# Decoding the first MLP's weight chunks in whole instead of in halves

## The chip, the cores and the metric

The kernel runs on one core of a Trainium2 chip. The metric is the device time of one execution in microseconds (us), given as the median of the runs.

## What is computed

Attention with a decay over 4 x 8 heads of 576 positions and 64 columns, whose output (2304 tokens x 512) goes through two MLPs. The inputs of the weights are float64.

```python
x = np.ascontiguousarray(attn_out.transpose(0, 2, 1, 3)).reshape(B * S, H * D)
# first MLP: w_in is 512 x 2048, w_out is 2048 x 512
h = x @ w_in
g = h - np.tanh(h)
x = g @ w_out
# second MLP: the same sizes
h = x @ w_in
r = np.maximum(h, 0.0)
out = (r * r) @ w_out
```

## The kernel before

Matrix products are made from a high and a low part of each operand (`PASSES`: high x high, high x low, low x high), so every operand is split: ScalarE rounds it to the high part, and a subtraction on VectorE or GpSimd gives the low part.

The first MLP's weights come in 16 chunks of 128 hidden columns. `load_w` brings a chunk with two DMAs on SyncE's queue: the w_in columns into the first half of the tile `wraw`, the w_out rows into the second half, as pairs of 32-bit words, two words for each float64. `decode_w` makes float32 numbers of them and then the two parts, in `w`. It works by halves of 512 numbers, first the w_in half (x = 0), then the w_out half (x = 1):

- `first(x)`: two ScalarE operations (L203, L204) take every second word each and shift it by a multiplication;
- `bits(x)`: two VectorE operations (L210, L212) put the fraction, the exponent and the sign together in the half of `wfull`;
- `parts(x)`: ScalarE makes the high part (L227), then the low part is made (L228) by GpSimd for the w_in half and by VectorE for the w_out half.

The tile `w` takes the place of `wraw`, so no part can be written before the last `bits` operation has read from there. `wfull` comes from a pair of buffers of 1024 columns (`wide`).

Order: the program is emitted by a clockwork. Each `cw.step` emits one piece of TensorE work (an atom) and counts one tick; `cw.later(k, fn)` emits `fn` k ticks later. `first(0)`, then 2 ticks (`LAG['wbits']`) to `bits(0)` and `first(1)`, 2 ticks to `bits(1)`, 3 ticks (`LAG['wparts']`) to `parts(0)`, 1 tick to `parts(1)`: 8 ticks for a chunk. A planner then orders the instructions of each engine, mainly by the order of emission, and places the semaphores; an engine runs its own list in order. A chunk's decode is begun by `feed.pace`, by how far TensorE's atoms of the first block of tokens are, or by `feed.upto` when a step of that block needs it. Before `h1_atoms` emits products with a chunk that is not in `ready_w`, it steps the clock until it is. The h products (L1017) read the w_in half (`win`), high part first; the y products (L1057) read the w_out half (`wout`).

In the same stage the first half of the attention's heads runs: GpSimd makes the decay rows Pb (L552, L556), VectorE takes the row maximum (L669), ScalarE the exponential (L678).

The second MLP's weights go through the same function with phase 1 and 2, later in the span.

Of the kernel before, what the change touches and what calls it, by code (L numbers as in the profile page):

```python
# [10 lines left out]
F32 = mybir.dt.float32  # L11
F32R = mybir.dt.float32r
U32 = mybir.dt.uint32
AF = mybir.ActivationFunctionType
ALU = mybir.AluOpType
# [4 lines left out]
NT, DM, DFF = B * S, H * D, 2048  # L20
P = 128
# [36 lines left out]
LAG = dict(max=2, exp=1, norm=3, tr=3, trlo=2, pv=1, pvadd=1, qk=1, qklo=1, th=1, sub=1, hi=1, lo=1, wbits=2, wparts=3,  # L58
           relu=1, sq=1, lo2=1, load=8)
# [51 lines left out]
def fused_kernel(ctx: ExitStack, tc: tile.TileContext, q, k, v, f, w1i, w1o, w2i, w2o, out):  # L111
    nc = tc.nc
    cw = Clockwork(tc)
# [3 lines left out]
    wp = ctx.enter_context(tc.tile_pool(name="wp", bufs=1))  # L117
# [15 lines left out]
    wraw, wt, ready_w = {}, {}, set()  # L133
# [12 lines left out]
    def pin(ins):  # L146
        if ordered:
            tc.keep_in_program_order(ins)
# [4 lines left out]
    def wide(name, dtype):  # L153
        return wp.tile([P, 1024], dtype, tag="wide", name=name, bufs=2)

    def load_w(phase, fc):
        if phase == 0:
            t = wp.tile([P, 2, 1024], U32, tag=f"w{fc}", name=f"wraw_{phase}_{fc}", bufs=1)
            src_in, src_out = wsrc[0]
            pieces = ((t[:, 0].rearrange("p (c f) -> p c f", c=ND),  # L160
                       src_in[:, 2 * fc * P : 2 * (fc + 1) * P].rearrange("(c p) f -> p c f", p=P)),
                      (t[:, 1], src_out[fc * P : (fc + 1) * P, :]))
        else:
            tag = SUMTAG[fc] if phase == 1 else 15
            t = wp.tile([P, 2, 1024], U32, tag=f"w{tag}", name=f"wraw_{phase}_{fc}", bufs=1)
            src_in, src_out = wsrc[1]
            if phase == 1:
                pieces = [(t[:, c].rearrange("p (c f) -> p c f", c=2),
                           src_in[2 * c * P : 2 * (c + 1) * P, 4 * fc * P : 4 * (fc + 1) * P]
                           .rearrange("(c p) f -> p c f", p=P)) for c in range(2)]  # L170
            else:
                pieces = [(t[:, c], src_out[(2 * fc + c) * P : (2 * fc + c + 1) * P, :]) for c in range(2)]
        wraw[phase, fc] = t
        for dst, src in pieces:
            (move if phase == 2 else load)(dst, src)
# [3 lines left out]
    def decoded():  # L179
        busy.pop()  # L180
        if pending:
            decode_w(*pending.pop(0))

    pending = []

    def decode_w(phase, fc):
        if phase:
            if busy:
                pending.append((phase, fc))
                return  # L190
            busy.append((phase, fc))
        raw = wraw.pop((phase, fc)).rearrange("p i d -> p (i d)")
        pair = raw.rearrange("p (d t) -> p d t", t=2)
        full = wide(f"wfull_{phase}_{fc}", U32)
        w = 512

        spots = ((full[:, :w], full[:, w:]), (raw[:, :w], raw[:, w : 2 * w]))

        def first(x):
            lo_, hi_ = spots[x]  # L200
            words = pair[:, x * w : (x + 1) * w]

            pin(nc.scalar.activation(lo_, words[:, :, 0], AF.Copy, scale=0.936 * 2.0 ** -29))  # L203
            pin(nc.scalar.activation(hi_.bitcast(F32), words[:, :, 1].bitcast(F32), AF.Copy, scale=2.0 ** -112))  # L204
            cw.later(LAG['wbits'], lambda: bits(x))

        def bits(x):
            lo_, hi_ = spots[x]
            dst = full[:, x * w : (x + 1) * w]
            nc.vector.scalar_tensor_tensor(lo_, in0=hi_, scalar=3, in1=lo_,  # L210
                                           op0=ALU.logical_shift_left, op1=ALU.bitwise_or)
            nc.vector.scalar_tensor_tensor(dst, in0=hi_, scalar=0x80000000, in1=lo_,  # L212
                                           op0=ALU.bitwise_and, op1=ALU.bitwise_or)
            if x == 0:
                first(1)
            else:
                if phase == 2 and fc + 1 < NP2:
                    cw.later(1, lambda: load_w(2, fc + 1))
                cw.later(LAG['wparts'], (lambda: parts(0)) if phase == 0 else (lambda: combine(phase, fc, full)))

        def parts(x):
            if x == 0:
                wt[phase, fc] = wp.tile([P, 2, 2, DM], F32R, tag=f"w{fc}", name=f"w_{phase}_{fc}", bufs=1)
            t = wt[phase, fc]
            hi, lo = (t[:, hl].rearrange("p i d -> p (i d)")[:, x * w : (x + 1) * w] for hl in range(2))
            src = full[:, x * w : (x + 1) * w].bitcast(F32)
            nc.scalar.activation(hi, src, AF.Copy)  # L227
            (nc.vector if x else nc.gpsimd).tensor_tensor(lo, in0=src, in1=hi.bitcast(F32), op=ALU.subtract)  # L228
            if x == 0:
                cw.later(1, lambda: parts(1))  # L230
            else:
                ready_w.add((phase, fc))

        first(0)
# [880 lines left out]
    class Feed:  # L1115
# [11 lines left out]
        def one(self):  # L1127
            assert self.decoded < self.loaded
            decode_w(*self.items[self.decoded])
            self.decoded += 1  # L1130
# [164 lines left out]
    for fn, what in (  # L1295
            (lambda p: decode_w(2, p), {0: 20, 1: 34, 2: 48, 3: 62, 4: 76, 5: 90, 6: 104, 7: 118}),
            (lambda i: stage_load(i), {1: 9, 2: 64}),
            (lambda i, x: y_sum(i, x), {(1, 0): 22, (1, 1): 25, (1, 2): 32, (1, 3): 36,
                                        (2, 0): 75, (2, 1): 79, (2, 2): 89, (2, 3): 93}),
            (lambda p: final_load(p), {0: 121, 1: 122, 2: 134, 3: 141, 4: 148, 5: 150, 6: 152, 7: 172}),  # L1300
            (lambda p: final_split(p), {0: 128, 1: 136, 2: 143, 3: 148, 4: 157, 5: 168}),
            (lambda n: g_load(n), {0: 138, 1: 145, 2: 165, 3: 170}),
            (lambda n: g_sums(n), {0: 146, 1: 154, 2: 171}),
            (lambda hl: g_split_first(hl), {0: 159, 1: 161}),
            (lambda e: g_split_second(e), {0: 165, 1: 167})):
        for arg, at in what.items():
            events.setdefault(at, []).append((fn, arg))
# [250 lines left out]
```

## Time and profile before

| | |
|---|---|
| median of 3 runs | 1008.18 us (1006.85 to 1009.23) |
| the profiled execution | 1005.81 us |
| its span in the trace | 1004.1 us |
| TensorE busy | 977.4 us |
| VectorE busy | 722.0 us |
| ScalarE busy | 627.1 us |
| GpSimd busy | 356.3 us |
| HBM traffic over the span | 140 GB/s |

PE is TensorE's matmul, PEld its weight load, DVE is VectorE, ACT ScalarE, POOL GpSimd, SP SyncE. Busy time is the time in which an engine had an instruction in work; instructions that follow one another directly overlap a little, so two durations add up to more than the time from the first start to the second end. An idle time stands with the instruction that ended it and with what released that instruction.

### The profile page before, as it was taken

To read this page: it belongs to the slowest core of one execution; us is meant where nothing else is said; L and a number is where in the kernel's file an instruction comes from. 1 tells how busy PE (TensorE), PEld (TensorE's weight loads), DVE (VectorE), ACT (ScalarE), POOL (GpSimd) and SP (SyncE) were. 2 spreads that over 40 slices of the span, in tenths; PEclk is the share of its full clock that TensorE was granted. 3 is DMA by queue.
4 is the path that set the end of the run, shared out by engine and by line. 5 is a ranking of instruction groups with operands and counts; after the bars stand their busy time and mean duration, and the time that the engine had idled before them with its cause. 6 is when DMAs were issued, how large, how long until landed. Compare 5 with 4: busy or idle time off the path is not lost.

```text
span 1004.1 us, 19916 instructions
## 1 busy us (share of the span) xinstructions
PE 977.4 (97%) x6990; PEld 929.5 (93%) x6990; DVE 722.0 (72%) x1513; ACT 627.1 (62%) x1249; POOL 356.3 (35%) x511
## 2 busy tenths in 40 slices
PE   7989999999999999999999999999999999999998
PEld 5778889999999999999999877999999999999998
DVE  4897884587878877878753589755447569987773
ACT  5896874566666666665643367767666767655551
POOL 4664453455566655565510343342323000000000
PEclk9999999999999999999999999999999999999999
DMA  8946744363353444443201432576877974544431
GB/s 235 272 137 228 217 112 100 107 140 82 101 142 91 115 120 102 113 120 93 75 20 36 153 127 84 162 258 222 282 272 247 331 229 118 168 141 134 127 106 42
DMA packets 220004, 149.58 MB, mean 149 GB/s; under 512 B 116384, under 2 KB 197600, under 8 KB 219904
## 3 DMA queue, kind: packets, MB, share of 16 engines
q1 hardware_dynamic: 219856, 148.28, 50.3%
q8 instruction: 55, 0.90, 0.4%
q14 instruction: 45, 0.37, 0.1%
q10 hardware_dynamic: 48, 0.03, 0.0%
HBM read 101.00 MB, written 39.92 MB: 140 GB/s over the span
## 4 chain that ended last, share of the span: by engine, by line
PE 68%; DVE 10%; ACT 3%; issue 2%; DMA 1%; SPq 1%; POOL 1%; DVEq 0%; ACTq 0%; POOLq 0%
PE o L1394 17%; PE r L1226 15%; PE h L1017 14%; PE y L1057 14%; PE pv L858 3%; PE pt L775 2%; DVE KL L630 2%; PE s L740 2%; DVE PT L785 2%; PE s L742 1%; DVE Pb L669 1%; DVE g L1030 1%; DVE ghl L1038 1%; DVE wq L321 1%; PE pv L820 1%
## 5 line engine op out<-in xcount | busy, mean ns | idle before, releaser
L1057 PE MATMUL y<-ghl,w 128*128 128x256 f32 (+1 forms) x1536 | 241.2, 301 | 1.5 <-DVE ghl L1038 1.5
L1057 PEld LDWEIGHTS y<-ghl,w 128*128 128x128 f32 x1536 | 209.5, 191 | 13.4 <-DVE ghl L1038 3.3
L1017 PE MATMUL h<-x,w 128*128 128x256 f32 x1344 | 199.2, 291 | 5.5 <-POOL w L228 4.7
L1017 PEld LDWEIGHTS h<-x,w 128*128 128x128 f32 x1344 | 175.9, 192 | 12.8 <-POOL w L228 6.3
L1394 PE MATMUL o<-ws,gc 128*128 128x256 f32 x864 | 116.0, 283 | 0.0
L1394 PEld LDWEIGHTS o<-ws,gc 128*128 128x128 f32 x864 | 109.2, 192 | 0.0
L1226 PE MATMUL r<-yt,ws 128*128 128x384 f32 x576 | 106.6, 336 | 0.5 <-ACT g L1244 0.5
L1226 PEld LDWEIGHTS r<-yt,ws 128*128 128x128 f32 x576 | 100.0, 188 | 2.9 <-ACT g L1244 2.5
L1394 PE MATMUL o<-wq,gc 128*128 128x256 f32 x648 | 90.9, 284 | 1.7 <-DVE gc L1360 1.5
L694 POOL TENSOR_SCALAR Pb<-Pb,st 128x384 f32<-128x384 f32 (+2 forms) x80 | 58.0, 726 | 81.1 <-DVE st L688 60.7
L1394 PEld LDWEIGHTS o<-wq,gc 128*128 128x128 f32 x648 | 83.5, 192 | 2.5 <-DVE gc L1360 1.9
L669 DVE CUSTOM_DVE_ANT_0 Pb<-s,Pb 128x128 f32<-128x128 f32 (+4 forms) x144 | 66.9, 482 | 22.1 <-PE s L742 13.8
L678 ACT ACTIVATE Pb<-Pb,st 128x384 f32<-128x384 f32 (+2 forms) x80 | 55.2, 689 | 42.8 <-DVE st L669 42.0
L1226 PE MATMUL r<-yt,wq 128*128 128x384 f32 x432 | 80.1, 335 | 0.3 <-ACT g L1244 0.2
L1030 DVE TENSOR_TENSOR g<-h,g 128x512 f32<-128x512 f32 x72 | 49.4, 686 | 42.5 <-ACT g L1027 41.8
L1360 DVE TENSOR_TENSOR gc<-graw,gc 128x1792 fp32r<-128x1792 f32 x34 | 68.7, 2022 | 13.5 <-ACT gc L1356 13.5
L1226 PEld LDWEIGHTS r<-yt,wq 128*128 128x128 f32 x432 | 75.1, 188 | 1.3 <-ACT g L1244 1.1
L1356 ACT ACTIVATE gc<-graw 128x1792 fp32r<-128x1792 f32 x34 | 57.7, 1697 | 28.0 <-PE o L1394 17.6
L256 POOL TENSOR_TENSOR wsum<-wfull 128x256 f32<-128x256 f32 x32 | 29.9, 935 | 118.5 <-DVE wfull L212 95.3
L1237 DVE TENSOR_TENSOR g<-r,g 128x384 f32<-128x384 f32 x71 | 39.0, 553 | 42.3 <-PE r L1226 23.3
L1027 ACT ACTIVATE g<-h 128x512 f32<-128x512 f32 x72 | 42.7, 592 | 40.2 <-PE h L1017 39.6
L1034 ACT ACTIVATE ghl<-g 128x512 fp32r<-128x512 f32 x72 | 45.4, 630 | 34.6 <-DVE g L1030 33.9
(155 smaller groups left out, 1879.1 us busy)
## 6 DMA issues: line engine op xcount, KB each, us to landing
graw<-gscr SPq DMA_DIRECT2D x144, 128.0 KB, 2.6
gscr<-g SPq DMA_DIRECT2D x95, 192.0 KB, 3.6
wraw<-in_moe_w_in_dram SPq DMA_DIRECT2D x32, 512.0 KB, 4.6
wraw<-in_moe_w_out_dram SPq DMA_DIRECT2D x32, 512.0 KB, 5.5
neg<-cscr SPq DMA_DIRECT2D x32, 288.0 KB, 3.4
v<-in_v_dram SPq DMA_DIRECT2D x48, 128.0 KB, 2.8
qk<-in_k_dram SPq DMA_DIRECT2D x64, 72.0 KB, 2.4
K<-K SPq DMA_DIRECT2D x32, 144.0 KB, 3.0
```

Source lines behind the costliest of these rows:

```text
L669: nc.vector.tensor_tensor_reduce(out=d, in0=t[:rows, src : src + m], in1=d, scale=-0.125, scalar=3.0e38 if j == 0 else stat(0, x)[:rows], ...
L678: nc.scalar.activation(d, d, AF.Exp, bias=stat(len(parts) - 1, x)[:rows], scale=-1.0, accum_out=stat(2, x)[:rows])
L694: nc.gpsimd.tensor_scalar(d, d, r, 1.0, op0=ALU.mult, op1=ALU.mult)
L1017: nc.tensor.matmul(o, lhsT=win(fc, wh, dc), rhs=xpart(j, dc, xh), start=dc == 0 and wh + xh == 0, stop=dc == ND - 1 and wh == 1)
L1027: pin(nc.scalar.activation(g, t, AF.Tanh))
L1030: pin(nc.vector.tensor_tensor(g, t, g, op=ALU.subtract))
L1034: pin(nc.scalar.activation(ghl[:, 0], g, AF.Copy))
L1057: nc.tensor.matmul(o, lhsT=wout(fc, wh, i * P, P), rhs=ghl[:, xh, fj * n : fj * n + n], start=s == 0 and fj == 0 and wh + xh == 0 and i % ...
L1226: nc.tensor.matmul(t, lhsT=wprod(1, p, k, wh)[:, dc * P : (dc + 1) * P], rhs=yt[i, k][:, xh, dc], start=k in FRESH and dc == 0 and wh + xh ...
L1356: pin(nc.scalar.activation(hi, t[:, 1:8], AF.Copy))
L1360: pin(nc.vector.tensor_tensor(lo, in0=t[:, 1:8], in1=hi.bitcast(F32), op=ALU.subtract))
L1394: nc.tensor.matmul(o, lhsT=gc[n][gh, e][:, GWHERE[k]] if n == 1 else gc[n][gh][:, GWHERE[k], e], rhs=wprod(2, 2 * q + e, k, wh), start=q = ...
```

## The change

The first MLP's chunks go through a new function, `decode_first`; `decode_w` keeps the second MLP's. A chunk is decoded in whole: two ScalarE operations of 1024 columns read every second word of the whole tile (the second one writes into the tile's own first half), two VectorE operations of 1024 put the bits together, one ScalarE operation of 1024 makes the high part, and one tick later both low parts are emitted, GpSimd's for the first 512 columns and VectorE's for the last 512. The ticks are 2, 3 and 1.

```diff
+    def decode_first(fc):
+        raw = wraw.pop((0, fc)).rearrange("p i d -> p (i d)")
+        words = raw.rearrange("p (d t) -> p d t", t=2)
+        full, hi_ = wide(f"wfull_0_{fc}", U32), raw[:, :1024]
+        nc.scalar.activation(full, words[:, :, 0], AF.Copy, scale=0.936 * 2.0 ** -29)
+        nc.scalar.activation(hi_.bitcast(F32), words[:, :, 1].bitcast(F32), AF.Copy, scale=2.0 ** -112)
+
+        def bits():
+            nc.vector.scalar_tensor_tensor(full, in0=hi_, scalar=3, in1=full,
+                                           op0=ALU.logical_shift_left, op1=ALU.bitwise_or)
+            nc.vector.scalar_tensor_tensor(full, in0=hi_, scalar=0x80000000, in1=full,
+                                           op0=ALU.bitwise_and, op1=ALU.bitwise_or)
+            cw.later(LAG['wparts'], parts)
+
+        def parts():
+            t = wt[0, fc] = wp.tile([P, 2, 2, DM], F32R, tag=f"w{fc}", name=f"w_0_{fc}", bufs=1)
+            hi, lo = (t[:, hl].rearrange("p i d -> p (i d)") for hl in range(2))
+            src = full.bitcast(F32)
+            nc.scalar.activation(hi, src, AF.Copy)
+
+            def low():
+                for eng, c in ((nc.gpsimd, slice(0, 512)), (nc.vector, slice(512, 1024))):
+                    eng.tensor_tensor(lo[:, c], in0=src[:, c], in1=hi[:, c].bitcast(F32), op=ALU.subtract)
+                ready_w.add((0, fc))
+            cw.later(1, low)
+        cw.later(LAG['wbits'], bits)
+
     def decode_w(phase, fc):
+        if phase == 0:
+            return decode_first(fc)
```

## Rows read from the trace of the kernel before

**Rows 1.** The page: busy time (share, instructions), and PEld in 40 slices, tenths.

```profile
PE 977.4 (97%) x6990; PEld 929.5 (93%) x6990; DVE 722.0 (72%) x1513; ACT 627.1 (62%) x1249; POOL 356.3 (35%) x511
...
PEld 5778889999999999999999877999999999999998
```

**Rows 2.** Stretches: length, busy us (instructions) of PE, PEld, DVE, ACT, POOL; clock, DMA, GB/s.

```profile
42.00:133.00 91.00, 84.84 (x606) 75.20 (x604) 79.14 (x177) 73.84 (x178) 47.89 (x58) 0.94 0.63 194
...
150.00:175.00 25.00, 25.00 (x215) 24.53 (x213) 12.08 (x31) 12.13 (x31) 7.02 (x15) 1.00 0.45 97
...
50.00:58.00 8.00, 4.85 (x34) 3.80 (x33) 7.86 (x15) 8.00 (x21) 7.40 (x9) 0.99 0.41 113
58.00:66.00 8.00, 7.91 (x50) 7.45 (x51) 8.00 (x17) 6.43 (x16) 2.53 (x3) 0.79 0.43 142
```

**Rows 3.** Waits of PEld, 42 to 134 us: us in total, times, longest.

```profile
PEld h L1017 <- POOL w L228: 6.3, 7, 1.6
...
PEld h L1017 <- ACT w L227: 1.5, 3, 0.8
```

**Rows 4.** Timeline, chunks 14 and 15: start, us, engine, line, operation [idle before].

```profile
124.74 0.70 ACT L203 ACTIVATE wfull<-wraw 128x512 uint32<-128x512 uint32 x1
...
126.92 0.69 DVE L212 SCALAR_TENSOR_TENSOR wfull<-wfull 128x512 uint32<-128x512 uint32 x1
126.98 1.78 POOL L228 TENSOR_TENSOR w<-wfull,w 128x512 fp32r<-128x512 f32 x1 [2.95 <-ACT w L227]
...
127.53 1.78 DVE L228 TENSOR_TENSOR w<-wfull,w 128x512 fp32r<-128x512 f32 x1
...
131.16 1.16 ACT L227 ACTIVATE w<-wfull 128x512 fp32r<-128x512 f32 x2 [0.17 <-DVE wfull L212]
...
131.87 1.28 POOL L228 TENSOR_TENSOR w<-wfull,w 128x512 fp32r<-128x512 f32 x1 [0.54 <-ACT w L227]
...
132.35 1.35 DVE L228 TENSOR_TENSOR w<-wfull,w 128x512 fp32r<-128x512 f32 x1 [0.60 <-ACT w L227]
...
133.20 0.89 PEld L1017 LDWEIGHTS h<-x,w 128*128 128x128 f32 x7 [0.77 <-POOL w L228]
```

**Rows 5.** The decode's operations up to 140 us: ns min/median/max, first and last start.

```profile
L227 ACT ACTIVATE w<-wfull x32: 612/622/641, 25.4 to 131.7; 128x512 fp32r<-128x512 f32 x32
L203 ACT ACTIVATE wfull<-wraw x16: 642/670/697, 12.5 to 124.7; 128x512 uint32<-128x512 uint32 x16
...
L210 DVE SCALAR_TENSOR_TENSOR wfull<-wfull x16: 670/686/878, 13.8 to 126.1; 128x512 uint32<-128x512 uint32 x16
...
L228 POOL TENSOR_TENSOR w<-wfull,w x14: 1276/1416/1780, 46.3 to 131.9; 128x512 fp32r<-128x512 f32 x14
...
L228 DVE TENSOR_TENSOR w<-wfull,w x16: 679/834/1781, 27.9 to 132.3; 128x512 fp32r<-128x512 f32 x16
...
  DMA wraw<-in_moe_w_in_dram: 4.2, 2
```

**Rows 6.** 1024-wide operations elsewhere in the span, by line and shape: busy us, mean ns.

```profile
L1336 ACT ACTIVATE graw<-graw 128x1024 f32<-128x1024 f32 x36 | 38.0, 1057 | 38.1 <-DMA graw<-gscr 38.1
...
L320 ACT ACTIVATE ws<-wst 128x1024 fp32r<-128x1024 f32 x5 | 5.3, 1055 | 0.0
L321 DVE TENSOR_TENSOR ws<-wst_s,ws 128x1024 fp32r<-128x1024 f32 x3 | 3.7, 1221 | 1.5 <-ACT ws L320 1.5
```

**Rows 7.** Chunk 8: the issues on the timeline, us to landing, ScalarE's first operation.

```profile
62.98 0.45 SPq L140 DMA_DIRECT2D wraw<-in_moe_w_in_dram  x1
...
63.48 0.82 SPq L140 DMA_DIRECT2D wraw<-in_moe_w_out_dram  x1
...
wraw<-in_moe_w_in_dram SPq DMA_DIRECT2D x1, 512.0 KB, 7.9
wraw<-in_moe_w_out_dram SPq DMA_DIRECT2D x1, 512.0 KB, 8.7
...
71.02 0.69 ACT L203 ACTIVATE wfull<-wraw 128x512 uint32<-128x512 uint32 x1 [0.36 <-DMA wraw<-in_moe_w_in_dram]
```

## The prediction

> **What bounds the kernel now.** I read the page first: TensorE is busy for 97% of the span and its weight loads for 93%, but the loads stand at five to eight tenths in the first six of forty slices and then at nine, but for three slices around 600 us [rows 1]. So most of what another engine can still give back lies in the first 150 us, and the changed function works only there, from 12.5 us to 133 us [rows 5]. Next come the stretches. From 42 us (about where the first MLP's products begin) to 133 us (the last chunk is ready) TensorE's loads are busy 75.2 of 91 us, against 24.53 of 25 just behind; VectorE is busy 79.1 and ScalarE 73.8 of the 91, the granted clock is 0.94 of its full level, and in 50 to 66 us VectorE has nothing free at all (7.86 and 8.00 of 8.00) [rows 2]. So this stage is bound by a mesh: ScalarE and VectorE nearly full, and TensorE waiting for what they hand over.
>
> How much of that waiting is the decode's? In the same stretch the weight loads of the h products stand idle 6.3 us for GpSimd's low parts (seven times) and 1.5 us for ScalarE's high parts (three times) [rows 3]. These 7.8 us are what the change can reach directly.
>
> **One chunk, as it runs now.** Chunk 15: ScalarE starts it at 124.74, GpSimd's low part starts at 131.87 and takes 1.28, the product starts at 133.20 [rows 4]. That is 8.4 us to the end of the low part. With each operation at its own duration and nothing in the way: two ScalarE halves 1.21 (1.16 for two high parts back to back, and 0.05 more, since a half that reads every second word takes 0.67 against 0.62), two VectorE halves 1.29 (126.92 to 127.53 is 0.61 from start to start, plus 0.68), both again for the second half, a high part 0.62, the low part 1.28 [rows 4, 5]: 6.9 us. The other 1.5 us are queues at five hand-overs.
>
> **Part 1, wider operations.** The change makes three ScalarE operations of 1024 out of six of 512, two VectorE bit operations out of four, and leaves the low parts at 512. A 1024-wide copy on ScalarE takes 1.06 in two groups, two halves back to back 1.16 [rows 4, 6]: 0.10 us saved per pair, 0.3 a chunk, 4.8 over 16. For the pairs that read every second word I keep the 0.05 more for the whole too. On VectorE a 1024-wide operation with two inputs takes 1.22 undisturbed [rows 6], two halves 1.29: 0.07 saved per pair, 0.14 a chunk, 2.2 over 16. No row has a 1024-wide bit operation; the halves cost the same as a 512-wide subtraction (0.68), so the range is 0 to 0.14 per pair. Taken on an engine that is full, this is worth its sum at most: 14 chunks fall between 46 and 133 us, so 4.2 us of ScalarE and 2.0 us of VectorE [rows 5].
>
> **Part 2, a shorter chain.** The new chain, with nothing in the way: two whole ScalarE operations 2.1, two whole VectorE operations 2.4, high part 1.06, low part 1.28: 6.8 us, as good as the 6.9 now. What goes is two of five hand-overs, each worth 0.3 us by chunk 15: 0.9 left instead of 1.5, so a chunk is ready 0.7 us sooner. The emission says the same in its own unit: 2+2+3+1 = 8 ticks now, 2+3+1 = 6 then, so in the program a chunk's end stands two steps ahead of where it stood. But a product's first matmuls need only the high part, and that now comes as one operation of 1.06, not of 0.62: for the three waits on ScalarE 0.26 of the 0.7 is left. Taking 0.7 from each of the seven waits on GpSimd gives 4.9; not each is that long (0.9 on average, 1.6 the longest [rows 3]), so 4.5. With 0.26 from each of the three on ScalarE, 0.8, it is 5.3 us of 7.8.
>
> This sum isn't all kept. TensorE that is early by one wait meets the next chunk early too, and a chunk is started by ScalarE and VectorE, so what accumulates is limited by what these engines get ahead: 2.0 us on VectorE, 4.2 on ScalarE. Between 2.0 and 5.3 I take the middle, 3.6.
>
> **Part 3, both low parts at once.** The rows say they don't run at once. At 127.53 VectorE's low part was issued while GpSimd's ran until 128.76: it took 1.78 instead of 0.68 and ended 0.55 after GpSimd. At 132.35 the same: 1.35, and 0.55 after GpSimd's 133.15. The other way round, GpSimd's at 126.98 took 1.78 instead of 1.28, because VectorE's bit operation had begun at 126.92 [rows 4]. So whoever comes second stands still, and the pair takes 1.28 + 0.55 = 1.83 us from its release in either order. The Trainium skill states the mechanism (SBUF — State Buffer, Who interferes with whom): VectorE with two SBUF inputs and a GpSimd operation that reads SBUF share one port pair, under an exclusive lock that the first one keeps for its whole instruction. The trace agrees with it (1.78 against 0.68). If they could run side by side, a chunk's low parts would be ready 0.55 us sooner than in the sum made here.
>
> The cost: VectorE's low part has a minimum of 0.68, a median of 0.83 and a maximum of 1.78 [rows 5]. Issued beside GpSimd's every time, it lies between -0.15 (VectorE always first) and +0.95 us per chunk (always second) from the median: -2 to +13 us of VectorE over 14 chunks. I take +0.3, nearer the median, because when VectorE is behind with its queue some other operation of two inputs is the one that stands still, as now. That is 4 us of VectorE time against 2.0 saved; it counts where VectorE has nothing free, which the rows show for 16 of the 91 us: 16/91 of 4, 0.7 us. Where VectorE comes first, GpSimd's low part and the product behind it are late by 0.5; that is in the range.
>
> **Part 4, the first operation waits for both loads.** Now the first half reads only the w_in rows, the second only the w_out rows. A whole needs both. Chunk 8: w_in is issued at 62.98 and lands 7.9 later, at 70.9, and ScalarE, which waited for it, starts at 71.02; w_out is issued at 63.48 and lands after 8.7, at 72.2 [rows 7]. ScalarE would stand still 1.2 us more there, with the softmax's exponentials and the tanh behind it. Two waits on such loads show in all [rows 5]. I take 0 for these, since ScalarE has 17 us free in the stretch [rows 2], and keep 1.2 each, 2.4 us, for the range.
>
> What is moved besides: the wide buffer and the raw tile are freed two ticks sooner, and no DMA, semaphore queue or order of loads changes. The order within each engine follows from the order of emission and a planner, so the rest of the span shifts a little as well; no row bounds this, I allow 2 us either way.
>
> **Sum.** 3.6 - 0.7 = 2.9, about 3 us off the span: 1004.1 to 1001.1. The profiled execution took 1005.81 (1.7 beyond its span) and would take 1002.8; the median of the runs, 1008.18, lies 2.4 above it, so the median becomes 1005.2.
>
> **The rivals.**
> *More than that.* All 7.8 us of waits vanish, and with them part of what the lowered clock costs: 0.94 over 91 us is 5.5 us at the full level, and the deepest drop, 0.79 of 8 us, follows directly on the longest standstill, 50 to 58 us, where TensorE was busy only 4.85 of 8 [rows 2]. With 2 of the 5.5 us: 10 us, 998. Against it: ScalarE and VectorE can't get 10 us ahead.
> *Nothing.* The waits change their name. VectorE is full in 50 to 66, its own load hardly falls (2 saved, up to 4 added), and TensorE waits for the ghl or x parts instead of w. 1008, within 2. For it: VectorE is the fuller of the two engines; against it: 7.8 us of idle time have w as their releaser.
> *Slower.* The port pair. If VectorE's low part is second nearly always, it costs 0.95 a chunk, 13 us over the 14, less 2.0: 11 us, against 11.9 us that VectorE has free in the stretch [rows 2], and these are not free where needed. Half of it reaching TensorE gives 5.5 us, 1013.5. It decides from about 0.5 us a chunk on (7 us less 2.0 on VectorE, half of it 2.5, as much as the forecast gains), that is a mean low part of 1.3 us.
> That the change doesn't do what it says (no overlap) is part 3, and in all four cases.
>
> **How the numbers follow.** Forecast (about 1005.2, from 1001 to 1006) 0.40; more 0.10; nothing 0.26; slower 0.24. The range from 999.5 to 1012 leaves out the far ends of the first and the last rival. A measurement of this kernel tells 0.2% (2 us) from no change; with that bound the cases give faster 0.50, same 0.26, slower 0.24.
>
> **What would show it.** Right: the last low part ends before 132.5 instead of 133.15; the h products' idle time for w falls from 7.8 to about 3; ScalarE's busy time in the stage falls by 4 us or more; 1024-wide operations at 1.06 to 1.11 and 1.22. Part 3: VectorE's w low parts at a mean of about 1.1 to 1.3; at 1.6 the slower rival holds. Part 4: waits of ScalarE for the w_out load, where none is now. Wrong: the idle time for w falls and the last chunk is no sooner, or the difference arises behind 133 us, where the planner's order and not the decode made it.

## The result: slower by 0.8%

The changed kernel takes 1016.49 us (median of 7 runs, 1013.19 to 1018.38) against 1009.23 us for the kernel before on the same chip (7 runs, 1006.85 to 1013.92). The ratio is 1.0076, with a 95% interval from 1.0057 to 1.0095. The forecast was 1005.2 us, the range ended at 1012: the sign was wrong. The profiled execution took 1017.04 us with a span of 1014.9, 10.8 us more than the span of before; that is more than the ratio's 7.7, since the profiled execution of before (1005.81) was faster than its seven. An execution more than 1.5% above the fastest of its kernel is in no ratio below (two of ten in e6, four of ten in e8, one of twelve each in e14 and e15); with them the means put e6 and e14 at 0.995 and e8 at 1.010.

Each execution also has a mean granted clock of TensorE, and the time goes with it. Beside the experiments the kernel before took 1010.1 us on average at 0.990 (12 executions) and 1009.7 at 0.991 (20). The kernel after took 1015.17 at 0.990 and 1013.37 at 0.991. So 4 to 5 us of the loss are there at the same clock, and the rest comes with a lower one.

The page of the kernel after, its busy times and two of its rows of 40 slices (the answer to [rows 1]):

```profile
PE 986.4 (97%) x6990; PEld 937.2 (92%) x6990; DVE 718.4 (71%) x1481; ACT 622.5 (61%) x1201; POOL 357.3 (35%) x511
...
PEld 5778879999899999999999877899999999999998
...
PEclk9779999999999999999999999999999999999999
```

VectorE and ScalarE have less to do by 3.6 and 4.6 us, as the change intends, and the span is longer all the same. The stretches of [rows 2], and one more (same columns):

```profile
42.00:133.00 91.00, 83.59 (x562) 74.04 (x563) 68.72 (x141) 62.99 (x125) 44.02 (x55) 0.89 0.60 184
150.00:175.00 25.00, 25.00 (x212) 24.07 (x212) 14.76 (x45) 13.54 (x40) 6.20 (x15) 1.00 0.46 108
50.00:58.00 8.00, 6.59 (x52) 5.78 (x53) 7.69 (x17) 5.59 (x9) 4.05 (x4) 1.00 0.64 189
58.00:66.00 8.00, 5.84 (x29) 4.66 (x28) 7.56 (x10) 6.82 (x14) 4.24 (x5) 0.75 0.11 29
...
34.70:48.40 13.70, 13.70 (x57) 10.90 (x56) 8.89 (x30) 8.21 (x23) 7.25 (x16) 0.50 0.95 268
```

From 42 to 133 us TensorE gets through 562 matmuls instead of 606, with the clock at 0.89 instead of 0.94, and every helper engine is emptier. Nobody is full; they wait for one another.

Where the 10.8 us arise can be read off the h products on the timeline. The first one starts at 46.2 us (before: 42.0). From there to the 192nd, the last of the first block of tokens, it takes 99.0 us (before: 92.3). From there to the last h product of the first MLP it takes 498.1 (before: 497.0). So 4.2 us are lost before the first product, 6.7 in the stage in which the chunks are decoded, and almost nothing behind it. In that stage the weight loads stand idle 18.4 us instead of 14.2; the rest is slower work, with the clock at its lower level for 17.1 us of the stage instead of 10.2. In this execution the start has the clock at 0.50, its 1.2 GHz level, from 34.7 to 48.4 us (last row above).

What the weight loads of h wait for, in the kernel after from 42 to 145 us (the answer to [rows 3]; engine and line, releaser: us in total, times, longest):

```profile
PEld h L1046 <- POOL w L208: 7.8, 8, 2.9
...
PEld h L1046 <- ACT w L204: 2.2, 2, 1.7
```

That is 10.0 us instead of 7.8, and the longest wait for GpSimd is 2.9 instead of 1.6. So 2.2 of the 4.2 us of added idle time have w as their releaser. The decode's operations in the kernel after, up to 150 us (ns min/median/max, as in [rows 5]):

```profile
L190 ACT ACTIVATE wfull<-wraw x16: 1108/1143/1187, 14.6 to 133.9; 128x1024 uint32<-128x1024 uint32 x16
...
  DMA wraw<-in_moe_w_out_dram: 1.0, 1
...
L204 ACT ACTIVATE w<-wfull x16: 1041/1056/1060, 27.3 to 140.5; 128x1024 fp32r<-128x1024 f32 x16
...
L194 DVE SCALAR_TENSOR_TENSOR wfull<-wraw,wfull x16: 1197/1226/1843, 18.2 to 136.3; 128x1024 uint32<-128x1024 uint32 x16
...
L208 POOL TENSOR_TENSOR w<-wfull,w x16: 1264/1494/1944, 28.4 to 141.7; 128x512 fp32r<-128x512 f32 x16
L208 DVE TENSOR_TENSOR w<-wfull,w x16: 671/692/1776, 34.6 to 141.6; 128x512 fp32r<-128x512 f32 x16
```

The widths cost what was forecast. VectorE's low part got no longer: over 42 to 145 us its mean is 1.04 us, against 1.05 before. GpSimd's own duration is little longer (1.54 us in the mean, 1.46 before). What is late, in some chunks, is its start. One chunk of the kernel after, number 11 (the first is 0), rows of its timeline (the chunk's first operation is at 104.00; the operations at 110.00 and 111.74 are the next chunk's, and the row at 114.01 holds the low parts of both chunks, 1.26 us the first):

```profile
104.00 1.15 ACT L190 ACTIVATE wfull<-wraw 128x1024 uint32<-128x1024 uint32 x1
105.54 1.13 ACT L191 ACTIVATE wraw<-wraw 128x1024 f32<-128x1024 f32 x1
105.58 0.82 POOL L581 TENSOR_SCALAR Pb<-neg,ccol 128x128 f32<-128x128 f32 x2
...
106.76 1.23 DVE L194 SCALAR_TENSOR_TENSOR wfull<-wraw,wfull 128x1024 uint32<-128x1024 uint32 x1 [0.57 <-ACT wraw L191]
...
108.50 1.22 DVE L196 SCALAR_TENSOR_TENSOR wfull<-wraw,wfull 128x1024 uint32<-128x1024 uint32 x1
...
109.80 1.05 ACT L204 ACTIVATE w<-wfull 128x1024 fp32r<-128x1024 f32 x1
...
110.00 1.23 DVE L194 SCALAR_TENSOR_TENSOR wfull<-wraw,wfull 128x1024 uint32<-128x1024 uint32 x1
...
111.14 0.69 DVE L208 TENSOR_TENSOR w<-wfull,w 128x512 fp32r<-128x512 f32 x1
...
111.56 2.00 POOL L581 TENSOR_SCALAR Pb<-neg,ccol 128x128 f32<-128x128 f32 x2 [4.68 <-DMA neg<-cscr]
...
111.74 1.22 DVE L196 SCALAR_TENSOR_TENSOR wfull<-wraw,wfull 128x1024 uint32<-128x1024 uint32 x1
...
113.64 0.41 POOL L585 TENSOR_SCALAR_AFFINE_SELECT Pb<-Pb 128x256 f32<-128x256 f32 x1
...
114.01 2.97 POOL L208 TENSOR_TENSOR w<-wfull,w 128x512 fp32r<-128x512 f32 x2
...
115.33 1.24 PEld L1046 LDWEIGHTS h<-x,w 128*128 128x128 f32 x10 [2.92 <-POOL w L208]
```

The high part is done at 110.85. GpSimd's low part starts 3.2 us later, because two decay rows and a select stand ahead of it on its queue. Three things add up: the decay rows wait for their own load (`neg`) until 111.56, 0.7 us; they take 2.00 us (0.82 where nothing holds them, at 105.58), while VectorE's three operations with two inputs from 110.00 to 112.96 follow one another without a gap; and the select takes the rest. So 1.2 of the 3.2 us are time in which GpSimd is held, and 2.0 are its queue. TensorE stands 2.92 us for it. The chunk takes 11.3 us from its first operation to the end of its low part.

This does not happen to every chunk. Of chunks 2 to 15, ten have GpSimd's low part done 1.35 to 2.03 us behind the high part, as before (1.36 to 1.98). Four are late: 5.5 and 2.5 us (chunks 7 and 8), 4.4 and 2.9 (11 and 12). In chunk 7, too, decay rows that had waited for their load stand ahead; the first of them takes 2.83 us. The low parts of 8 and 12 stand behind those of 7 and 11:

```profile
81.36 3.28 POOL L581 TENSOR_SCALAR Pb<-neg,ccol 128x128 f32<-128x128 f32 x2 [2.09 <-DMA neg<-cscr]
...
85.09 2.52 POOL L208 TENSOR_TENSOR w<-wfull,w 128x512 fp32r<-128x512 f32 x2
```

Chunk 7's lateness cost TensorE 0.17 us, since its products were not due yet; the 2.92 us for chunk 11 are the one wait for GpSimd in this trace that is longer than the longest of before (1.6).

The kernel before, the chunk at the same place, the ScalarE and VectorE rows of its timeline:

```profile
113.03 0.67 ACT L203 ACTIVATE wfull<-wraw 128x512 uint32<-128x512 uint32 x1
113.60 0.65 ACT L204 ACTIVATE wfull<-wraw 128x512 f32<-128x512 f32 x1
...
114.67 0.68 ACT L203 ACTIVATE wraw<-wraw 128x512 uint32<-128x512 uint32 x1
...
114.91 0.69 DVE L210 SCALAR_TENSOR_TENSOR wfull<-wfull 128x512 uint32<-128x512 uint32 x1
...
115.23 0.68 ACT L204 ACTIVATE wraw<-wraw 128x512 f32<-128x512 f32 x1
```

Here VectorE joins the bits of the first half (114.91) while ScalarE reads the second (114.67 to 115.91). That overlap inside a chunk is gone in the kernel after. Taken over chunks 2 to 15, a chunk's mean time from its first ScalarE operation to the end of its w_in low part is 9.36 us before and 11.37 after: 7.72 and 9.08 to the end of the w_in high part, 1.64 and 2.29 from there.

### The profile page after: what moved, and what is told of

It is laid out like the page before. It is cut to its first block, busy times and chain, and to the rows that moved or that the text cites. A ratio compares the mean times of both kernels' runs of the same rounds, so it can differ in the third digit from the quotient of the medians.

```text
span 1014.9 us, 19817 instructions
## 1 busy us (share of the span) xinstructions
PE 986.4 (97%) x6990; PEld 937.2 (92%) x6990; DVE 718.4 (71%) x1481; ACT 622.5 (61%) x1201; POOL 357.3 (35%) x511
## 4 chain that ended last, share of the span: by engine, by line
PE 67%; DVE 13%; issue 6%; ACT 5%; POOL 3%; DMA 3%; SPq 1%; POOLq 0%; DVEq 0%; ACTq 0%
PE o L1423 16%; PE h L1046 14%; PE y L1086 13%; PE r L1255 12%; PE pv L887 3%; PE pt L804 2%; PE s L769 2%; DVE PT L814 2%; DVE KL L659 2%; PE s L771 1%; DVE g L1059 1%; DVE ghl L1067 1%; DVE Pb L698 1%; POOL w L208 1%; POOL Pb L581 1%
## 5 line engine op out<-in xcount | busy, mean ns | idle before, releaser
L1086 PE MATMUL y<-ghl,w 128*128 128x256 f32 (+1 forms) x1536 | 244.3, 303 | 1.5 <-DVE ghl L1067 1.5
L1086 PEld LDWEIGHTS y<-ghl,w 128*128 128x128 f32 x1536 | 211.9, 193 | 13.6 <-DVE ghl L1067 3.3
L707 ACT ACTIVATE Pb<-Pb,st 128x384 f32<-128x384 f32 (+2 forms) x80 | 55.2, 690 | 42.9 <-DVE st L698 42.2
```

The costliest lines, as they stand in the source:

```text
L707: nc.scalar.activation(d, d, AF.Exp, bias=stat(len(parts) - 1, x)[:rows], scale=-1.0, accum_out=stat(2, x)[:rows])
L1086: nc.tensor.matmul(o, lhsT=wout(fc, wh, i * P, P), rhs=ghl[:, xh, fj * n : fj * n + n], start=s == 0 and fj == 0 and wh + xh == 0 and i % ...
```

## The experiments

Two theories stood at the beginning. S: the loss is made at the start, by chunks 0 and 1, and by the lowered clock there. P: every whole chunk costs, by the port pair (in the forecast's slower rival, by VectorE's low part being held) and by longer operations ahead of others. The traces of e1 and e3 brought a third. Q: the other side of the same lock, GpSimd held by VectorE's operations, its low part late and h waiting. Its rival O, named with e5: the order that the planner makes for whole chunks is worse in itself, and GpSimd only shows it. All ratios are to the kernel before on the same chip (e1 to e4 and e13 to e16 ran on one chip, e5 to e12 on another), with 95% intervals.

| label | kernel | ratio | interval |
|---|---|---|---|
| e1 | after, chunks 0 and 1 in halves | 1.0081 | 1.0048 to 1.0114 |
| e2 | before, chunks 0 and 1 in whole | 1.0029 | 1.0010 to 1.0048 |
| e3 | after, more filling matmuls | 1.0103 | 1.0062 to 1.0143 |
| e4 | before, more filling matmuls | 0.9966 | 0.9943 to 0.9988 |
| e5 | after, the two low parts swapped | 1.0029 | 1.0010 to 1.0049 |
| e6 | after, both low parts on VectorE | 0.9962 | 0.9925 to 0.9999 |
| e7 | after, each 1024 as two 512 | 1.0058 | 1.0022 to 1.0094 |
| e8 | after, bit operations a tick apart | 1.0034 | 1.0013 to 1.0054 |
| e9 | before, both low parts on VectorE | 1.0002 | 0.9983 to 1.0022 |
| e10 | before, both low parts in one tick | 0.9976 | 0.9954 to 0.9998 |
| e11 | after, low parts a tick apart | 1.0099 | 1.0065 to 1.0133 |
| e12 | e6, more filling matmuls | 0.9985 | 0.9966 to 1.0005 |
| e13 | e6, GpSimd's subtraction back, unread | 1.0090 | 1.0058 to 1.0122 |
| e14 | e6 again | 0.9943 | 0.9926 to 0.9961 |
| e15 | e6, an unread GpSimd subtraction, 12 chunks | 1.0035 | 1.0015 to 1.0054 |
| e16 | as e15, on the chunk before | 1.0014 | 0.9992 to 1.0037 |

### Is it the start? (e1 to e4)

e1 leaves chunks 0 and 1 to the old way, e2 gives only these two to the new one.

```diff
-        if phase == 0:
+        if phase == 0 and fc >= 2:   # e1
+        if phase == 0 and fc < 2:    # e2
```

> Chunks 0 and 1 (decoded at the start, beside the first softmaxes) in halves as before, the other 14 in whole. In the changed kernel TensorE's first h product starts 4.3 us late (46.2 against 42.0) behind 13.7 us at the lower clock from about 34.7 us on, and another 6 us are lost between 46 and 143 us. Theory S (the start: the whole chunks 0 and 1 put the first softmaxes out of step, TensorE stands still, its clock falls): the first product is back at 42 to 43, no lowered clock before it, and the loss against the kernel before is at most 4 us, about half. Theory P (each whole chunk costs, by the port pair and by longer operations ahead of others): 14 of 16 chunks still cost, so a loss of 7 us or more.

> The converse: chunks 0 and 1 in whole, the other 14 in halves as before. Theory S: first product at 46 or later, lowered clock for 10 us or more ahead of it, a loss of 4 us or more. Theory P: a loss of about 1 us (2 chunks of 16).

e1 is as slow as the kernel after (1.0081), its first h product at 45.3 us, and its h products wait 12.6 us for GpSimd (longest 3.9). e2 loses 0.29%: its profiled execution was its slowest (1019.5, the others from 1009.3), with the clock at its 1.2 GHz level for 27.3 us from 26.4 us on. So chunks 0 and 1 cost some 0.3% by the start, and the other fourteen make the whole loss without them.

e3 and e4 put five filling matmuls into two more of the first heads' steps, on the kernels after and before.

```diff
-FILL = {4: 5}
+FILL = {4: 5, 6: 5, 8: 5}
```

> The changed kernel, with five more matmuls on constant data at two more places of the first attention units (i = 6 and i = 8), some 2.2 us of TensorE's time at the full clock. Theory S in its clock form: the clock stays up between 25 and 50 us, the first product starts by 44, and the time falls 2 to 5 us below the changed kernel. If the lowered clock is only a symptom of TensorE waiting: no gain, or 2 us slower.

> The kernel before with the same ten extra matmuls, as the control of the run above: its clock is already up there, so all theories expect no change or up to 2 us slower.

The kernel before gains 0.34%, where no change was expected; the kernel after gains nothing (1.0103). S is not the cause of the 0.8%. e3's trace shows Q more plainly than that of the kernel after (timeline, one chunk; high part done at 111.14):

```profile
110.09 1.05 ACT L204 ACTIVATE w<-wfull 128x1024 fp32r<-128x1024 f32 x1
...
110.22 1.40 DVE L194 SCALAR_TENSOR_TENSOR wfull<-wraw,wfull 128x1024 uint32<-128x1024 uint32 x1 [0.52 <-ACT wraw L191]
...
110.59 3.19 POOL L581 TENSOR_SCALAR Pb<-neg,ccol 128x128 f32<-128x128 f32 x2
...
111.54 0.68 DVE L208 TENSOR_TENSOR w<-wfull,w 128x512 fp32r<-128x512 f32 x1
...
112.14 1.30 DVE L196 SCALAR_TENSOR_TENSOR wfull<-wraw,wfull 128x1024 uint32<-128x1024 uint32 x1
...
114.24 1.26 POOL L208 TENSOR_TENSOR w<-wfull,w 128x512 fp32r<-128x512 f32 x1
...
115.55 1.78 PEld L1046 LDWEIGHTS h<-x,w 128*128 128x128 f32 x8 [3.77 <-POOL w L208]
```

Two decay rows take 3.19 us instead of 0.82. They end 0.3 us behind the third of VectorE's operations, and the low part that is queued behind them ends 4.4 us after its input was ready.

### Width, or the simultaneous low parts? (e7, e8, e10, e11)

e7 keeps the order and the ticks of the kernel after and makes each 1024-wide operation of two of 512 (ScalarE's three and VectorE's two). e8 and e11 move ticks: e8 puts one tick between the two bit operations, e11 puts GpSimd's low part into the tick of the high part and VectorE's one tick later. e10 gives the kernel before what the change's last words say, and nothing else: both high parts in one tick, both low parts in the next.

```diff
+        for c in (slice(0, 512), slice(512, 1024)):                 # e7, at each operation
+            nc.scalar.activation(full[:, c], words[:, c, 0], ...)
...
+            cw.later(1, sign)                                       # e8, before L196
+        def sign():
...
-            cw.later(LAG['wparts'], parts)
+            cw.later(LAG['wparts'] - 1, parts)
...
-            cw.later(1, low)
+            low(nc.gpsimd, slice(0, 512))                           # e11
+            cw.later(1, last)                                       # VectorE's low part
...
-                cw.later(1, lambda: parts(1))
+                parts(1)                                            # e10, in decode_w
...
+                cw.later(1, low)                                    # GpSimd's, then VectorE's
```

> The changed kernel's ticks and order of emission, with every 1024-wide operation emitted as two of 512: only the width differs. Theory Q in its width form (one operation of 1.22 holds GpSimd off twice as long as one of 0.68): decay rows on GpSimd over 2 us disappear and 4 us or more come back. If the run of VectorE operations counts and not the width of one, or by rival O: within 3 us of the changed kernel.

> The changed kernel with its two VectorE bit operations emitted one tick apart (ticks 2, 1, 2, 1, the same 6 in all), so that other VectorE work can stand between them. Theory Q: shorter runs, the single longest GpSimd operation falls from about 3.2 to under 2.5 us, a gain of 2 us or more. Rival O: any change of order is as good as another, so a gain or a loss without shorter standstills.

> The part 'at the same time' alone: the kernel before, in halves as it was, but both high parts in one tick and both low parts (GpSimd's and VectorE's) in the next; still 8 ticks. If issuing the two low parts together does the harm (VectorE's goes first, GpSimd's comes late): 3 us slower or more, standstills of h behind GpSimd longer than 2.5 us. If the harm comes from both bit operations of a whole chunk standing in a row on VectorE: no change within 2 us.

> The converse: the changed kernel in whole chunks, but GpSimd's low part emitted right behind the high part and VectorE's one tick later; still 6 ticks. If issuing them together does the harm: 4 us or more faster than the changed kernel. If the row of bit operations does it: within 3 us of the changed kernel, and GpSimd's decay rows still take over 2.5 us at times.

e7 stays slow (1.0058, h waits 9.4 us for GpSimd, longest 3.1): not mainly the width, but the order in which a whole chunk is decoded. e10 isn't slow at all (0.9976, h waits 6.3 us for GpSimd, longest 1.6, as in [rows 3]), but it does not test what it was made for. Its edit moved the ticks, and the planner put the operations back nearly where they had been: up to 160 us GpSimd's list is that of the kernel before, VectorE's differs in the place of one low part and a few others between 63 and 82 us, and in eight of chunks 2 to 15 the two low parts start as far apart as before, to 0.01 us. e11 did not move them apart either (1.0099; its profiled execution also had the clock low for 27.3 us): in seven of the fourteen chunks VectorE's low part starts within 0.1 us of GpSimd's, against four in the kernel after. So whether the simultaneous low parts do harm by themselves is not shown by any run. e8 seems to give back about half (1.0034, from six executions), yet its trace has a wait of 4.3 us for GpSimd, and its longest GpSimd operation takes 3.22 us, where Q expected under 2.5: that speaks for O more than for Q, and does not settle it.

### Who is in the way? (e5, e6, e9, e12, e14)

e5 swaps the engines of the two low parts, so that GpSimd's goes to the y products and VectorE's to h. e6 leaves GpSimd out: one VectorE subtraction of 1024 columns. e14 is e6 again, and e12 is e6 with the filling of e3. e9 makes both low parts on VectorE in the kernel before.

```diff
-                for eng, c in ((nc.gpsimd, slice(0, 512)), (nc.vector, slice(512, 1024))):
+                for eng, c in ((nc.vector, slice(0, 512)), (nc.gpsimd, slice(512, 1024))):   # e5
+                for eng, c in ((nc.vector, slice(0, 1024)),):                                # e6, e12, e14
...
-            (nc.vector if x else nc.gpsimd).tensor_tensor(lo, ...)
+            (nc.vector if x or phase == 0 else nc.gpsimd).tensor_tensor(lo, ...)             # e9
```

> The changed kernel with the low parts exchanged: VectorE makes those of w_in (the h products wait for them), GpSimd those of w_out (the y products, later). In the changed kernel and in the two runs above with whole later chunks, the longest standstills of h (2.5 to 4.3 us each) end with GpSimd's low part, which came 2 to 3 us after its high part was there, behind decay rows of 0.4 us that took up to 3.2 us beside two 1024-wide bit operations and a low part of VectorE in a row. Theory Q (GpSimd starves behind such runs and h waits for GpSimd): no standstill of h over 2 us is left between 42 and 145 us, their sum falls from 10 to 4 us or less, and the time falls by 5 us or more, to within 3 us of the kernel before. Rival O (the order that the planner makes for whole chunks is worse in itself, GpSimd only shows it): h then waits for VectorE's low parts as long, and the time stays within 3 us of the changed kernel.

> The changed kernel with both low parts in one VectorE operation of 1024 (some 1.22 us), none on GpSimd. Theory Q: as in the run above, waits of h for a low part 4 us or less, a gain of 3 us or more on the changed kernel, less than the exchange if VectorE's 0.6 us more per chunk count. Rival O: within 3 us of the changed kernel, or slower by VectorE's added 0.6 x 14 = 8 us.

> The kernel before with all 32 low parts of the first MLP's weights on VectorE (two of 512 a chunk), none on GpSimd. The whole chunks gained 1.4% when their low parts left GpSimd. Theory Q (GpSimd's low part, behind its decay rows and VectorE's runs, sets when h can start, and whole chunks only make this worse): the kernel before gains too, but less, 0.1% to 0.5% (1 to 5 us), since its standstills behind GpSimd were 6.3 us with 1.6 the longest; and whole chunks are then no slower than halves. Rival O (what was gained is special to the order of whole chunks): the kernel before stays the same or loses by VectorE's added 8 us.

> Whole chunks with the low parts on VectorE, and the ten extra matmuls in the attention's start that gained 0.3% in the kernel before. In the profile of the kernel without them the clock was lowered only once, for 3.4 us at 52 us; so if they help by the clock, the gain is small: 0 to 3 us on that kernel, 4 to 8 us on the kernel before.

> The kernel of e6 once more, on the same chip and beside the same runs of the kernel before as e13, in five rounds. If whole chunks with the low parts on VectorE are really faster than the kernel before: 0.994 to 0.998. If e6 was a lucky order of a few runs: 0.999 to 1.002, and then the two tilings are alike once GpSimd is out of the way.

e5 takes h off GpSimd and gives back 0.5% of the 0.8 (1.0029); h's waits for w fall from 10.0 to 5.2 us, the longest is 1.6. e6 and e14 take GpSimd out and give back all of it and more: 0.9962 and 0.9943. The whole chunks are thus faster than the halves, once GpSimd has no part in them. On the kernel before the same edit is worth nothing (e9, 1.0002, where Q expected a gain of 0.1 to 0.5%), and h waits for high parts instead, 6.3 us. Set side by side: halves with GpSimd 1, halves without 1.0002, wholes with GpSimd 1.0076, wholes without 0.9943 to 0.9962. Neither the whole chunks nor GpSimd's part costs anything alone; the two together do. e12 adds the filling to e6 and gains nothing (0.9985, 0.2 to 0.4% slower than e6 and e14). Edits that have nothing to do with GpSimd thus move the time by a few tenths of a per cent (e4, e12), so half a per cent (e5, e8) is a weak answer, and 1.1 to 1.3% is not. e14, weight loads of h and VectorE's decode operations (42 to 145 us the waits, 25 to 145 the groups: busy us, mean ns):

```profile
PEld h L1046 <- DVE w L208: 2.5, 4, 1.2
...
PEld h L1046 <- ACT w L204: 1.6, 3, 1.2
...
L208 DVE TENSOR_TENSOR w<-wfull,w 128x1024 fp32r<-128x1024 f32 x16 | 20.2, 1264 | 0.5 <-ACT w L204 0.3
L196 DVE SCALAR_TENSOR_TENSOR wfull<-wraw,wfull 128x1024 uint32<-128x1024 uint32 x16 | 19.7, 1233 | 0.0
L194 DVE SCALAR_TENSOR_TENSOR wfull<-wraw,wfull 128x1024 uint32<-128x1024 uint32 x15 | 19.0, 1263 | 1.8 <-ACT wraw L191 1.7
```

There are 4.1 us of waits for w instead of 10.0, the last low part is done at 129.8 us instead of 143.5, and the first h product starts at 41.6. VectorE takes on 0.6 us a chunk for it.

### Does GpSimd harm where nobody waits for it? (e13, e15, e16)

e13 is e6 with GpSimd's subtraction back, its result written where nobody reads it. e15 does the same for chunks 0 to 11 without a buffer of the decode, and e16 reads the high part of the chunk before.

```diff
+                nc.gpsimd.tensor_tensor(src[:, :512], in0=src[:, :512], in1=hi[:, :512]..., op=ALU.subtract)   # e13
+                if fc < 12:                                                                       # e15; e16: 0 < fc < 13
+                    nc.gpsimd.tensor_tensor(spare, in0=old, in1=old, op=ALU.subtract)             # old: hi; e16: hi of fc - 1
```

> The kernel of e6 (whole chunks, both low parts in one VectorE operation of 1024), and behind it GpSimd makes the same subtraction over w_in's 512 columns once more, into the buffer of the whole chunk, which nobody reads after that. So GpSimd has its operation back (about 1.3 us, 16 of them) and holds the shared port as in the kernel after, but no product waits for it. If TensorE's wait for the late low part is the whole harm: as e6, 0.996 of the kernel before (within 0.003). If GpSimd's operations also harm by holding VectorE off and by pushing the decay rows back: between e6 and the kernel after, 1.000 to 1.007, with VectorE's operations longer (1024-wide subtraction above 1.22 us) and the decay rows late.

> The kernel of e6 (whole chunks, both low parts in one VectorE operation), and for chunks 0 to 11 one more GpSimd subtraction of 512 columns in the same tick, which reads the chunk's high part of w_in twice and writes into the place of chunk 15, free until its load. Nobody reads the result and no buffer of the decode is held by it (e13's held the wide buffer, and ScalarE waited 10.7 us for that). GpSimd still waits for the chunk's high part with its decay rows queued behind it, and holds the shared port for about 1.3 us, 12 times. If only TensorE's wait for a late low part harms: as e6 and e14, 0.994 to 0.997. If the queue or the port harm too: 0.998 to 1.004, and then e16 tells which.

> As e15, for chunks 1 to 12, but GpSimd's subtraction reads the high part of the chunk before, which is long there: GpSimd waits for nothing and holds no decay row up by waiting, only by the operation's own 1.3 us and by what VectorE holds it off. What is left is the shared port. If the port alone harms, as e15. If GpSimd's waiting in front of the decay rows was the harm in e15: as e6 and e14, 0.994 to 0.997. If both are at 0.994 to 0.997, the harm of GpSimd in the kernel after is TensorE's wait alone, and e13's loss is the held buffer.

e13 is the slowest but two (1.0090), but its trace shows a wait that the edit made: ScalarE's next first operation stood for the wide buffer, which GpSimd freed late (waits of ScalarE, 42 to 145 us):

```profile
ACT wfull L190 <- POOL wfull L209: 10.7, 5, 3.0
```

So e13 answers another question, what a late release of the wide buffer costs. e15 and e16 have no such hold, and they still lose 0.9% and 0.7% against e14 on the same chip (0.7% and 0.5% against e6, the same kernel as e14), by 12 operations that nobody reads. Up to 150 us VectorE, ScalarE and TensorE's loads run the list of e14 in its order, but for a few places exchanged between 34 and 40 us. So O is not the cause of this loss. e16, the waits of h (42 to 145 us), VectorE's operations (25 to 145) and GpSimd's waits (25 to 145):

```profile
PEld h L1056 <- DVE w L215: 6.1, 7, 2.0
...
L215 DVE TENSOR_TENSOR w<-wfull,w 128x1024 fp32r<-128x1024 f32 x16 | 23.4, 1460 | 0.5 <-ACT w L211 0.3
L203 DVE SCALAR_TENSOR_TENSOR wfull<-wraw,wfull 128x1024 uint32<-128x1024 uint32 x16 | 21.5, 1346 | 0.0
...
POOL spent L218 <- ACT w L211: 18.6, 5, 6.1
```

Here it is VectorE that is held: its low part takes 1.46 us instead of 1.26, the second bit operation 1.35 instead of 1.23, and h waits for the low part 6.1 us instead of 2.5. In e15 the same numbers are 1.48, 1.29 and 6.3. So both sides of the lock reach TensorE, each through the engine that makes h's low part: GpSimd in the kernel after, VectorE in e15 and e16. e16 was to keep GpSimd from waiting, and did not: the last row shows 18.6 us in which it stood for high parts with the decay rows behind it. The planner gave GpSimd the same list as in e15, and e16 is in effect e15 once more. Queue and port are therefore not told apart, and the two kernels' intervals overlap.

## Why the prediction was wrong, point by point

**What bounds the kernel** stood: 6.7 of the 10.8 us arise in the stage that was named, and h's waits for w are the largest item of its idle time (10.0 of 18.4 us).

**Part 1, wider operations: right.** 1.06 and 1.14 us on ScalarE (forecast 1.06 and 1.11), 1.22 on VectorE (1.22). Over the whole span ScalarE has 4.6 us less to do (forecast 4.8 for 16 chunks) and VectorE 3.6 (forecast 2.2 saved by width, and 4 lost to the lock).

**Part 2, the shorter chain: the first step that failed.** It set a chunk's undisturbed sums side by side, 6.9 us by halves and 6.8 in whole. The 6.9 counted "both again for the second half", as if ScalarE and VectorE took turns. The timeline of before shows ScalarE on the second half while VectorE is on the first; without the 1.21 us that are hidden so, the old sum is 5.7, and the whole is 1.1 us longer, not 0.1 shorter. Measured to the end of the high part it is 1.36 longer (7.72 to 9.08). The ticks, 8 and 6, were read as confirming it; they are places in the emission, and time is made by the engines. So the 3.6 us that the shorter chain was to give had no source. In e14, without GpSimd, a chunk still takes 0.6 us longer in the mean of chunks 2 to 15 (9.36 to 9.94), and yet the kernel is faster; a chunk's longer chain is not what decides.

**Part 3, both low parts at once: the term that decided, and mis-sized.** The lock was read correctly from [rows 4], but the cost was charged to VectorE (0.7 us), whose low part did not change (1.04 us in the mean, 1.05 before; the 0.3 a chunk was counted from the median, 0.83). "Where VectorE comes first, GpSimd's low part and the product behind it are late by 0.5; that is in the range": this 0.5 is what failed. It took one pair of operations for the whole contest and left out GpSimd's queue. The low part was done 1.64 us behind its high part in the mean before and 2.29 after. The rise is made by four chunks of fourteen, up to 5.5 us: in two of them decay rows stood ahead of the low part while VectorE ran two-input operations with no gap between, and the next chunk's low part stood behind it each time; the other ten are as before. VectorE's longest unbroken stretch of such operations did not grow (6.6 us before, 4.1 after, from 25 to 145 us), so their length alone does not explain it. The Trainium skill says of this pair (SBUF — State Buffer, Who interferes with whom) that whichever starts first keeps the ports for its whole instruction and the other blocks fully; the trace agrees, with two decay rows at 3.19 us instead of 0.82 (e3). Nothing in it excludes that the loser loses several times in a row, and that was left out of the sum. e5 and e6 put a size on the term: taking h off GpSimd is worth 0.5% (e5), taking GpSimd out 1.1 to 1.3% (e6, e14), 11 to 13 us where the sum had 0.7. That the two low parts were emitted together is not shown to be the reason, since e10 and e11 did not change it.

**Part 4, the first operation waits for both loads: right.** One such wait, 1.0 us. The first decode also begins 2.1 us later (14.6 instead of 12.5 us, and in e14 too), which e14 shows to cost nothing: its first h product is as early as before.

**The sum and the rivals.** Of the 2.9 us forecast nothing came: h's waits for w rose by 2.2 us instead of falling by 5. *Nothing* did not hold. *Slower* had the sign, and 1013.5 us lay nearer than the forecast; its mechanism was the wrong side of the lock, and its condition, a mean low part of 1.3 us on VectorE, did not hold at 1.04. *More* foresaw that the clock multiplies a change of waiting; it did, the other way. Between the first and the 192nd h product the clock was at its lower level for 17.1 us instead of 10.2, 6.9 us at half speed, so at most 3.5 us; these are inside the 6.7 us of the stage, not beside them.

**What stays open.** The 4.2 us before the first h product in the profiled execution: kernels of whole chunks show it early (40.8 and 41.6 in e6 and e14, 42.9 in e7) or late (53.2 in e11), and kernels with the old chunks 0 and 1 are late too (45.7 in e4, 44.9 in e9, 45.3 in e1), so how much of it belongs to the change cannot be told from one profile each; e2's 0.29% is the only measure. How the rest divides between the queue and the port is open as well, and so is why GpSimd's part harms the wholes and not the halves; e9 was not followed up. e6 and the kernel after differ in VectorE's order too, so a share of e6's gain can be O's.

The version that beats both kernels is e6 and e14: the chunks in whole, both low parts in one VectorE operation, 0.9943 of the kernel before (0.9926 to 0.9961) in e14, 0.9962 in e6.

## What to carry to other kernels

Before merging halves into wholes, draw the halves on both engines: with them goes an overlap between the engines, and here the high part of a chunk came 1.36 us later although each wide operation cost what was forecast. Where two engines share a lock, cost it for each of them as the waiting one, with everything that stands ahead on its queue and with the other's longest unbroken run, and ask which of the two the bottleneck waits for. A fuller engine can be the better place: VectorE took 0.6 us more a chunk and the kernel became faster. And where a planner orders the operations, see in the trace that an edit of the emission has moved them before its time is taken for an answer: e10 and e11 hardly did.

## What the runs showed of the hardware

- GpSimd can be held through several operations of VectorE: two decay rows of 0.41 us each took 3.19 while VectorE did three two-input operations back to back, and ended 0.3 us behind the last of them (e3). In the kernel after one such row took 2.83.
- An operation on GpSimd that nobody reads is not free beside a busy VectorE: 12 of them, 17 to 18 us of GpSimd, cost 0.7 to 0.9% (e16, e15 against e14; 0.5 to 0.7 against e6, the same kernel), with VectorE's 1024-wide subtraction at 1.46 to 1.48 us instead of 1.26.
- A 1024-wide bit operation with two inputs takes VectorE 1.22 us, as a subtraction does; ScalarE's copy of every second word takes 1.14 at 1024 columns, against 1.06 for adjacent ones.
- TensorE's granted clock went to 0.50, its 1.2 GHz level, for 13.7 us in the kernel after (TensorE had stood still 0.72 us, just ahead of 33.5 us), and for 27.3 us in the profiled executions of e2 and e11; in the kernel before its lowered stretches were 3.4 us each.
